# One ring of three accumulator banks in place of two and one, renewed planner durations and a new search, in a three-part attention and mixing kernel

## The chip, the cores and the metric

The kernel runs on one core of a Trainium2 chip. Its engines are TensorE (PE in the profile; PEld is its weight load), VectorE (DVE), ScalarE (ACT), GpSimd (POOL) and SyncE (SP), which issues nearly all DMAs. The metric is the device time of one execution, in microseconds, as the median of repeated runs.

## What is computed

Four batches of 448 tokens pass through causal attention with 12 heads of width 64, then a token mixer and a channel mixer, then a gated channel mix. Cut to what matters, the reference is:

```python
scores = q @ k.T / sqrt(64);  scores[mask] = -1e9          # per head, 448 x 448
attn = exp(scores - max);  attn /= sum + 1e-9
x = concat_heads(attn @ v)                                  # 4 x 448 x 768
u = x + (relu(x.T @ w_tok1) @ w_tok2).T                     # token mixing
x = u + relu(u @ w_ch1) @ w_ch2                             # channel mixing
xk, xr = lerp(x, x_prev, mu_k), lerp(x, x_prev, mu_r)
out = sigmoid(xr @ w_r) * (relu(xk @ w_k)**2 @ w_v)
```

The weights arrive in 64-bit floats. The kernel splits each into a high and a low 32-bit part and forms most products from three matmuls.

## The kernel before

**Stages.** Phase 0 does attention, token mixing and, as filler, a part of the channel mixer; it ends at about 368 us. Phase 1 does the rest of the channel mixer and the gated mix. Heads go in 24 pairs of two. For a pair, TensorE transposes q and k (tile `pt`, line 866), makes the scores (`ps`, line 891 for batch 0, line 900 with three matmuls for the others), and DVE adds the mask and finds the row maximum (line 912), ACT takes the exponential (928), DVE the reciprocal of the sum (942), DVE or POOL multiply by it (`norm`, line 946). TensorE then transposes the normalized block in five groups of four (`et_tr`, tile `pe`, line 969), ACT or DVE copies each group to SBUF (`et_copy`, recorded at line 240), TensorE forms the value product (`pv`, 985), ACT or DVE copies it to `xT`, TensorE turns it back (`pn`, 1003), and ACT and DVE split it into `xh`. After each third pair the token mixer runs: `k1` (tile `ph`), `k2` (tile `pu`) and a DVE sum into `xT` (line 1139). `early_ch1` forms the first half of the channel mixer's hidden rows (tile `pd`) for batches 0 to 2 while later pairs run; `pd` needs a whole batch's token mixing, so there is none before about 88 us.

**PSUM.** Phase 0 splits the eight banks into `ps_m` (two banks in a ring for `pt`, `pv`, `pn`, `ph`, `pu`), `ps_t` (one bank, for `pe` alone), `ps_s` (four, scores) and `ps_d` (one, `pd`). A tile that takes a bank of a ring waits until the last reader of the tile that had it before is done.

**The order.** Every step is a planner's entry: a due time, an engine (some may go to either of two), a duration, what it reads and writes, and the rings it takes from. `walk` plays all engines forward and lets each engine take, of what can start now, the entry with the lowest rank. `LAT` is the delay until a result can be used by another engine. `schedule` first shifts some ranks by pseudo-random amounts, one set per number in the list `NUDGES`, for phase 0 only. The resulting order on each engine is written into the program, and the chip's engines then run it strictly in that order, each waiting on semaphores. So the durations and the list change only which instruction stands where, and on which of two engines.

Of the kernel before, what the change touches and what calls it, by code (L numbers as in the profile page):

```python
# [10 lines left out]
F32 = mybir.dt.float32  # L11
# [4 lines left out]
PSUM = bass.MemoryType.PSUM  # L16
# [4 lines left out]
def kernel(  # L21
# [68 lines left out]


    PE, ACT, DVE, POOL, SP, NONE = "PE", "ACT", "DVE", "POOL", "SP", "-"
    LAT = {PE: 0.24, ACT: 0.2, DVE: 0.16, POOL: 0.12, SP: 2.8, NONE: 0.0}
    MODE, STICK, WAIT = 0.1, 1.5, 0.08
    DMA_RATE = 270e3

# [19 lines left out]
    def walk(mine, rank):  # L116

        for x in mine:
            x.left, x.next, x.pre = 0, [], []
        for x in mine:  # L120
            for k in x.r:
                for y in makers[k]:
                    if y.phase == x.phase:
                        x.left += 1
                        y.next.append(x)
                    else:
                        x.pre.append((None, 0.0, done_at[id(y)]))
        avail = {e: [x for x in mine if e in x.alt and not x.left] for e in free}
        out = []

        def start_of(x, eng):
            s = free[eng]
            for e, here, end in x.pre:
                s = max(s, here if e == eng != SP else end)
            if eng == PE and x.mode != state["mode"]:
                s += MODE
            more = {}
            for k in x.u:
                if k in taken:
                    continue  # L140
                pool = k[0]
                order = freed.setdefault(pool, [])
                i = len(order) + more.get(pool, 0) - bufs[pool]
                more[pool] = more.get(pool, 0) + 1
                if i >= 0:
                    ends = [done_at.get(id(y)) for y in users[order[i]]]
                    if None in ends:
                        return None
                    s = max(s, max(ends) + 0.05)
            return s  # L150

        while len(out) < len(mine):
            best = None
            for e, xs in avail.items():
                cand = [(start_of(x, e), x) for x in xs]
                cand = [c for c in cand if c[0] is not None]
                if not cand:
                    continue
                first = max(min(c[0] for c in cand), free[e]) + WAIT
                s, x = min(  # L160
                    (c for c in cand if c[0] <= first),
                    key=lambda c: rank[id(c[1])] + (STICK if e == PE and c[1].mode != state["mode"] else 0),
                )

                if any(start_of(x, o) + c < s + x.alt[e] - 0.01 for o, c in x.alt.items() if o != e):
                    others = [c for c in cand if c[1] is not x and c[0] <= first]
                    if not others:
                        continue
                    s, x = min(
                        others,  # L170
                        key=lambda c: rank[id(c[1])] + (STICK if e == PE and c[1].mode != state["mode"] else 0),
                    )
                if best is None or s < best[0]:
                    best = (s, x, e)
            assert best is not None, "stuck"
            s, x, eng = best
            for e in x.alt:
                avail[e].remove(x)
            cost = x.alt[eng]
            for k in x.u:  # L180
                if k not in taken:
                    taken[k] = s
                    freed.setdefault(k[0], []).append(k)
            free[eng] = s + cost
            end = s + cost + LAT[eng]
            if eng == PE:
                state["mode"] = x.mode
            if eng == SP:
                free[SP] = s + 0.1
                state["dma"] = max(state["dma"], s) + cost  # L190
                end = state["dma"] + LAT[SP]
            done_at[id(x)] = end
            out.append((s, x, eng))
            for y in x.next:
                y.left -= 1
                y.pre.append((eng, s + cost, end))
                if not y.left:
                    for e in y.alt:
                        avail[e].append(y)
        return out  # L200

    NUDGES = tuple(4000000 + n for n in (
# [9 lines left out]
    ))  # L214

    def noise(seed, i):
# [5 lines left out]
    def nudge(rank, mine, seed):  # L222
        share = (0.005, 0.02, 0.1)[int(3 * noise(seed, 1))]
        width = (3.0, 8.0, 20.0)[int(3 * noise(seed, 2))]
        for i, x in enumerate(mine):
            if noise(seed, 2 * i + 3) < share:
                rank[id(x)] += width * (2 * noise(seed, 2 * i + 4) - 1)

    def schedule(phase):
# [19 lines left out]
    def split64(t, key, use, dest, src, pp, n, blocks=False, lead=0):  # L249
# [52 lines left out]
        u = [("raw", k), ("tmp", k)]  # L302
        op(t - lead, SP, dma(pp * n * 8), load, w=[("raw", k)], u=u[:1])
        op(t, ACT, 0.04 + 0.43 * g, magnitude, r=[("raw", k)], w=[("mag", k)], u=u)
        slow = 0.3 if state["phase"] == 0 else 0.0
        op(t, DVE, 0.1 + (0.66 + slow) * g, shift, r=[("mag", k)], w=[("bit", k)], u=u[1:])
        op(t, DVE, 0.1 + (1.0 + slow) * g, assemble, r=[("bit", k)], w=[("asm", k)], u=u)
        op(t, ACT, 0.04 + 0.38 * g, high, r=[("asm", k)], w=[key + ("hi",)], u=u[1:] + use)
# [484 lines left out]
    with ExitStack() as c0:  # L793
# [5 lines left out]
        sp = c0.enter_context(tc.tile_pool(name="sp", bufs=4))  # L799
        ep = c0.enter_context(tc.tile_pool(name="ep", bufs=4))  # L800
        etp = c0.enter_context(tc.tile_pool(name="etp", bufs=2))
        ps_m = c0.enter_context(tc.tile_pool(name="ps_m", bufs=2, space=PSUM))
        ps_t = c0.enter_context(tc.tile_pool(name="ps_t", bufs=1, space=PSUM))
        ps_s = c0.enter_context(tc.tile_pool(name="ps_s", bufs=4, space=PSUM))
        ps_d = c0.enter_context(tc.tile_pool(name="ps_d", bufs=1, space=PSUM))
        ud = c0.enter_context(tc.tile_pool(name="ud", bufs=1))
        bufs.update({
            "kn": 2, "qn": 2, "vn": 3, "k": 2, "q": 2, "ms": 4, "e": 4, "et": 2, "xT": 6, "xh": 1,
            "h1": 1, "m": 2, "t": 1, "s": 2, "d": 1, "ue": KD, "h": 2, "st": 4,
        })  # L810

        mask = tw.tile([CP, S], F32, name="mask")
# [27 lines left out]
        def pair(g):  # L840
# [121 lines left out]
            def et_tr(i):  # L962
                if "et" not in T:
                    T["et"] = etp.tile([CP, len(groups) * S], F32, tag="et", name="et")
                pe = T["pe", i] = ps_t.tile([128, 512], F32, tag="t", name="pe")
                for j, kc in groups[i]:
                    o = place[j, kc] - S * i
                    for c in range(kc, NCH):
# [53 lines left out]
            for i, nm in enumerate("kq"):  # L1022
                t = s0 + 0.6 * i
                pt = ("m", nm, g)
                op(t, PE, 0.4, turn, nm, r=[(nm + "n", g)], w=[("pt", nm, g)], u=[(nm + "n", g), pt, (nm, g)])
                op(t - EV, ACT, 0.43, turned_hi, nm, r=[("pt", nm, g)], w=[(nm + "hi", g)], u=[pt, (nm, g)])
                if whole:
                    continue
                op(t - EV, DVE, 0.55, turned_lo, nm, r=[(nm + "hi", g)], w=[(nm + "lo", g)], u=[pt, (nm, g)])
            both = [(nm + x, g) for nm in "kq" for x in (("hi",) if whole else ("hi", "lo"))]  # L1030
            for i, cs in enumerate(units):
                t = s0 + 2.5 + (0, 2.2, 4.6)[i]
                su = ("s", i, g)
                op(
                    t, PE, (0.6, 0.74, 0.32)[i] * (4 / 3 if whole else 1), score, i, r=both, w=[("sc", i, g)],
                    u=[("k", g), ("q", g), su], mode="R",
                )
                for c in cs:
# [9 lines left out]
                            w=[("ex", j, c, g)], u=[ms, ("e", j, g), ("st", g)],  # L1048
                        )
            op(  # L1050
                s0 + 9, DVE, 0.33, recip, r=[("ex", j, c, g) for j in range(2) for c in range(NCH)],
                w=[("rc", g)], u=[("st", g)],
            )
            for j in range(2):
                for i, c in enumerate((3, 0, 1, 2)):
                    op(
                        s0 + 9.1 + 2 * j + 0.1 * i, POOL, (0.43, 0.53, 0.6, 0.7)[c], norm, j, c,
                        r=[("rc", g)], w=[("no", j, c, g)], u=[("e", j, g), ("st", g)],
                        alt={DVE: (0.16, 0.24, 0.32, 0.4)[c]},
                    )  # L1060
            for i in range(5):
                t = s0 + 11 + i
                need = [("no", j, c, g) for j, kc in groups[i] for c in range(kc, NCH)]
                op(
                    t, PE, 0.4, et_tr, i, r=need, w=[("tr", i, g)],
                    u=[("t", i, g), ("et", g)] + [("e", j, g) for j in {j for j, _ in groups[i]}],
                )
                op(
                    t - EV, ACT, 0.43, et_copy, i, r=[("tr", i, g)], w=[("et", i, g)], u=[("t", i, g), ("et", g)],
                    alt={DVE: 0.55},  # L1070
                )
            op(
# [231 lines left out]
```

## Time and profile before

| | |
|---|---|
| Median of 3 runs | 957.39 us (956.06 to 958.03) |
| Profiled execution, its own time | 957.5 us |
| Its span, first to last instruction | 955.7 us |
| TensorE busy over the span | 931.7 us (97%) |
| DVE, ACT, POOL busy | 582.7, 449.3, 67.2 us |

The profiled execution lies within the runs shown. Between its span and its own time there are 1.8 us that no instruction fills.

### The profile page before, as it was taken

Reading aid. Unit: us, or ns where it says so; the run is one execution under the profiler, and the core shown is the slowest. Engines: PE = TensorE matmul, PEld = TensorE weight load, DVE = VectorE, ACT = ScalarE, POOL = GpSimd, SP = SyncE. Lnnn points to the kernel's source line nnn. Section 1 sums busy time; section 2 is a strip of 40 time slices with the busy share of each in tenths; the row PEclk is TensorE's granted clock in tenths of the full one; section 3 lists DMA queues with packets and bytes.
Section 4 is the critical chain, followed back from the end, with each engine's and each line's share of the span. In section 5 each row is a group of like instructions: output and inputs, shape, how many; then the busy total and the mean of one; then the engine's idle time right before and its main releaser. Section 6 shows DMA issues by size and latency. Waiting matters only on the chain.

```text
span 955.7 us, 15553 instructions
## 1 busy us (share of the span) xinstructions
PE 931.7 (97%) x5496; PEld 832.2 (87%) x5496; DVE 582.7 (61%) x1450; ACT 449.3 (47%) x1082; POOL 67.2 (7%) x150
## 2 busy tenths in 40 slices
PE   6899999999999999999999999999999999999998
PEld 3566788878887888999999999999999999999998
DVE  5899998984677436997962118979745424231221
ACT  6988868774668443453430104556654313020210
POOL 1231112200111000000000000000000000000000
PEclk9999999999999999999999999999999999999999
DMA  9545565563442212566692445977741404102031
GB/s 183 132 114 140 156 172 156 168 186 103 117 124 93 81 58 98 149 185 228 204 337 102 138 151 174 308 242 240 220 141 33 150 25 154 49 19 89 28 94 50
DMA packets 149806, 133.55 MB, mean 140 GB/s; under 512 B 89888, under 2 KB 136480, under 8 KB 149728
## 3 DMA queue, kind: packets, MB, share of 16 engines
q1 hardware_dynamic: 148800, 132.33, 45.8%
q8 instruction: 43, 0.70, 0.3%
q10 hardware_dynamic: 928, 0.23, 0.1%
q14 instruction: 35, 0.29, 0.1%
HBM read 95.82 MB, written 33.03 MB: 135 GB/s over the span
## 4 chain that ended last, share of the span: by engine, by line
PE 91%; DVE 4%; ACT 3%; DMA 1%; issue 1%; SPq 0%; POOL 0%; DVEq 0%; ACTq 0%; POOLq 0%
PE pr L349 7%; PE pr L351 7%; PE pr L350 7%; PE acc L350 6%; PE acc L351 6%; PE acc L349 6%; PE pe L969 4%; PE ph L350 4%; PE ph L349 4%; PE ph L351 4%; PE pk L349 4%; PE pk L350 4%; PE pk L351 4%; PE pv L985 4%; PE ps L900 3%; PE pd L349 3%
## 5 line engine op out<-in xcount | busy, mean ns | idle before, releaser
L928 ACT ACTIVATE e<-ms,nm 112x448 f32<-112x448 f32 (+3 forms) x192 | 100.3, 526 | 13.6 <-DVE nm L912 11.6
L350 PE MATMUL acc<-a,w 128*128 128x448 f32 x288 | 105.2, 365 | 0.0
L349 PE MATMUL acc<-a,w 128*128 128x448 f32 x288 | 105.2, 365 | 0.0
L351 PE MATMUL acc<-a,w 128*128 128x448 f32 x288 | 105.2, 365 | 0.0
L912 DVE CUSTOM_DVE_ANT_0 ms<-ps,mask 112x448 f32<-112x448 f32 (+3 forms) x192 | 77.8, 442 | 6.9 <-PE ps L900 4.0
L969 PE MATMUL pe<-ident,e 112*112 112x112 f32 x480 | 69.8, 267 | 9.3 <-ACT et L240 5.2
L969 PEld LDWEIGHTS pe<-ident,e 112*112 112x112 f32 x480 | 51.2, 135 | 27.6 <-ACT et L240 6.3
L240 ACT COPY et<-pe 112x448 f32<-112x448 f32 x106 | 56.4, 532 | 37.1 <-PE pe L969 36.7
L294 ACT CAST w<-tmp 128x384 fp32r<-128x384 f32 (+2 forms) x100 | 50.1, 502 | 47.5 <-DVE tmp L289 46.8
L349 PE MATMUL pr<-w,a 128*128 128x384 f32 x216 | 72.2, 334 | 0.0
L350 PE MATMUL pr<-w,a 128*128 128x384 f32 x216 | 72.2, 334 | 0.0
L351 PE MATMUL pr<-w,a 128*128 128x384 f32 x216 | 72.2, 334 | 0.0
L534 ACT ACTIVATE a<-pk 128x448 f32<-128x448 f32 x32 | 17.5, 546 | 116.0 <-PE pk L351 116.0
L268 ACT ACTIVATE tmp<-raw 128x384 f32<-128x384 f32 (+2 forms) x100 | 54.2, 544 | 36.5 <-DVE w L298 24.5
L350 PE MATMUL pk<-a,w 128*128 128x448 f32 x192 | 70.7, 368 | 0.0
L351 PE MATMUL pk<-a,w 128*128 128x448 f32 x192 | 70.7, 368 | 0.0
L349 PE MATMUL pk<-a,w 128*128 128x448 f32 x192 | 70.6, 368 | 0.0
L572 DVE TENSOR_TENSOR r<-pr,r 128x384 f32<-128x384 f32 x28 | 15.6, 558 | 76.3 <-PE pr L351 76.2
L946 POOL TENSOR_SCALAR e<-e,rc 112x112 f32<-112x112 f32 (+3 forms) x78 | 46.7, 613 | 217.2 <-DVE rc L942 145.7
L349 PE MATMUL pd<-a,w 128*128 128x448 f32 x144 | 59.3, 412 | 0.2
L349 PE MATMUL pr<-w,kk 128*128 128x384 f32 x176 | 58.8, 334 | 0.0
L351 PE MATMUL pr<-w,kk 128*128 128x384 f32 x176 | 58.8, 334 | 0.0
(109 smaller groups left out, 2204.0 us busy)
## 6 DMA issues: line engine op xcount, KB each, us to landing
raw<-in_moe_w_ch_dram SPq DMA_DIRECT2D x48, 384.0 KB, 3.3
h_d<-he SPq DMA_DIRECT2D x24, 448.0 KB, 2.9
a<-h_d SPq DMA_DIRECT2D x24, 448.0 KB, 5.0
y<-y_d SPq DMA_DIRECT2D x48, 224.0 KB, 4.4
a<-u_d SPq DMA_DIRECT2D x36, 224.0 KB, 3.7
raw<-in_moe_w_k_dram SPq DMA_DIRECT2D x16, 384.0 KB, 4.1
raw<-in_moe_w_v_dram SPq DMA_DIRECT2D x16, 384.0 KB, 5.0
vn<-in_v_dram SPq DMA_DIRECT2D x48, 112.0 KB, 2.7
```

The lines of the kernel that those rows point to most:

```text
L240: nc.scalar.copy(o, i) if by == ACT else nc.vector.tensor_copy(o, i)
L268: nc.scalar.activation(box["tmp"], box["raw"][:, :, 1].bitcast(F32), AF.Abs, scale=65536.0)
L294: nc.scalar.copy(dest()[0], box["tmp"])
L349: nc.tensor.matmul(o, lh, rh, start=start and i == 0, stop=False)
L350: nc.tensor.matmul(o, lh, rl, start=False, stop=False)
L351: nc.tensor.matmul(o, ll, rh, start=False, stop=stop and i == n - 1)
L900: nc.tensor.matmul(T["s", j, c], T["q"][r, x, qc], T["k"][r, y, :n], start=i == 0, stop=i == 2,)
L912: nc.vector.tensor_tensor_reduce(out=ms[:, :n], in0=T["s", j, c], in1=mask[:, S - n:], scale=-0.125, scalar=BIG, op0=ALU.add, op1=ALU.min, ...
L928: nc.scalar.activation(T["e", j][:, eoff[c]:eoff[c + 1]], T["ms", j, c][:, :n], AF.Exp, bias=T["nm"][:, j, c:c + 1], scale=-1.0, accum_out ...
L946: (nc.gpsimd if by == POOL else nc.vector).tensor_scalar(out=ec, in0=ec, scalar1=T["rc"][:, j, c:c + 1], scalar2=1.0, op0=ALU.mult, op1=AL ...
L969: nc.tensor.transpose(pe[:CP, o + (c - kc) * CP:o + (c - kc + 1) * CP], T["e", j][:, eoff[c] + kc * CP:eoff[c] + (kc + 1) * CP], ident[:CP ...
L985: nc.tensor.matmul(T["pv"][64 * j:64 * j + 64, kc * CP:S], T["vn"][:, kc, j, :], T["et"][:, o:o + S - kc * CP], start=kc == 0, stop=kc == 2,)
```

## The change

The ring of two and the single bank become one ring of three: `et_tr` now takes its tile from `ps_m`, in turn with `pt`, `pv`, `pn`, `ph` and `pu`. Durations in the planner are renewed: each DMA now occupies SP's issue for 0.5 us (1.0 us for the loads of q, k, v and u) instead of 0.1, the first pair's transposes and scores are taken as slower, the split of a weight in phase 0 as faster on DVE, and `norm` on DVE as slower by 0.07 to 0.15. The list of rank shifts is another one (76 numbers in place of 118), and steps due before -10 (the first loads) are no longer shifted.

```diff
-    LAT = {PE: 0.24, ACT: 0.2, DVE: 0.16, POOL: 0.12, SP: 2.8, NONE: 0.0}
+    LAT = {PE: 0.24, ACT: 0.2, DVE: 0.16, POOL: 0.12, SP: 2.6, NONE: 0.0}
...
-                free[SP] = s + 0.1
+                free[SP] = s + (1.0 if x.f[0].__name__ == "load" and x.u[0][0] != "raw" else 0.5)
...
-    NUDGES = tuple(4000000 + n for n in (
+    NUDGES = tuple(1000000 + n for n in (
...
-            if noise(seed, 2 * i + 3) < share:
+            if x.t > -10 and noise(seed, 2 * i + 3) < share:
...
-        slow = 0.3 if state["phase"] == 0 else 0.0
+        slow = 0.12 if state["phase"] == 0 else 0.0
...
-        ps_m = c0.enter_context(tc.tile_pool(name="ps_m", bufs=2, space=PSUM))
-        ps_t = c0.enter_context(tc.tile_pool(name="ps_t", bufs=1, space=PSUM))
+        ps_m = c0.enter_context(tc.tile_pool(name="ps_m", bufs=3, space=PSUM))
...
-            "h1": 1, "m": 2, "t": 1, "s": 2, "d": 1, "ue": KD, "h": 2, "st": 4,
+            "h1": 1, "m": 3, "s": 2, "d": 1, "ue": KD, "h": 2, "st": 4,
...
-                pe = T["pe", i] = ps_t.tile([128, 512], F32, tag="t", name="pe")
+                pe = T["pe", i] = ps_m.tile([128, 512], F32, tag="m", name="pe")
...
-                op(t, PE, 0.4, turn, nm, r=[(nm + "n", g)], w=[("pt", nm, g)], u=[(nm + "n", g), pt, (nm, g)])
+                op(t, PE, 0.9 if g == 0 else 0.4, turn, nm, r=[(nm + "n", g)], w=[("pt", nm, g)], u=[(nm + "n", g), pt, (nm, g)])
...
-                    t, PE, (0.6, 0.74, 0.32)[i] * (4 / 3 if whole else 1), score, i, r=both, w=[("sc", i, g)],
+                    t, PE, (0.6, 0.74, 0.32)[i] * (1.8 if g == 0 else 4 / 3 if whole else 1), score, i, r=both, w=[("sc", i, g)],
...
-                s0 + 9, DVE, 0.33, recip, r=[("ex", j, c, g) for j in range(2) for c in range(NCH)],
+                s0 + 9, DVE, 0.45, recip, r=[("ex", j, c, g) for j in range(2) for c in range(NCH)],
...
-                        alt={DVE: (0.16, 0.24, 0.32, 0.4)[c]},
+                        alt={DVE: (0.24, 0.31, 0.42, 0.55)[c]},
...
-                    u=[("t", i, g), ("et", g)] + [("e", j, g) for j in {j for j, _ in groups[i]}],
+                    u=[("m", "t", i, g), ("et", g)] + [("e", j, g) for j in {j for j, _ in groups[i]}],
```

On TensorE's queue in the first pairs, before, a group of `pe` (four transposes) mostly stands alone between other work; `ps` are scores, `pt` the transposes of q and k, `pv` the value product, `pn` the turn back:

```order
L985 MATMUL pv<-et,vn 64x224 x2
L969 MATMUL pe<-ident,e 112x112 x4
L891 MATMUL ps<-kt,qt 112x224 x2
L1003 MATMUL pn<-ident,xT 112x128 x4
L969 MATMUL pe<-ident,e 112x112 x4
L866 MATMUL pt<-ident,kn 128x112 x4
L969 MATMUL pe<-ident,e 112x112 x4
L866 MATMUL pt<-ident,qn 128x112 x4
L969 MATMUL pe<-ident,e 112x112 x4
L891 MATMUL ps<-kt,qt 112x448 x2
L969 MATMUL pe<-ident,e 112x112 x4
```

At the same place of the changed kernel (lines stand 5 lower) all five groups of the second pair follow each other:

```order
L980 MATMUL pv<-et,vn 64x224 x2
L886 MATMUL ps<-kt,qt 112x448 x2
L886 MATMUL ps<-kt,qt 112x336 x2
L886 MATMUL ps<-kt,qt 112x112 x2
L998 MATMUL pn<-ident,xT 112x128 x4
L964 MATMUL pe<-ident,e 112x112 x20
L886 MATMUL ps<-kt,qt 112x224 x2
L861 MATMUL pt<-ident,kn 128x112 x4
L861 MATMUL pt<-ident,qn 128x112 x4
L980 MATMUL pv<-et,vn 64x448 x2
```

So runs of transposes are longer. Counted over phase 0, TensorE's queue goes 120 times into or out of a run of scores or of value products before, and 108 times in the changed kernel; between transposes and the wide matmuls (`ph`, `pu`, `pd`) it goes 162 times before and 135 times after. The count of matmuls is the same, 5256.

At TensorE's border between the phases, before, nine matmuls of the channel mixer (`ph` from line 349 to 351, first three blocks of u) stand ahead of the last token-mixing product `pu`:

```order
L351 MATMUL pu<-w_129,h_4787 128x448
L349 MATMUL ph<-a,w 128x448
L350 MATMUL ph<-a,w 128x448
L351 MATMUL ph<-a,w 128x448
L349 MATMUL ph<-a,w 128x448
L350 MATMUL ph<-a,w 128x448
L351 MATMUL ph<-a,w 128x448
L349 MATMUL ph<-a,w 128x448
L350 MATMUL ph<-a,w 128x448
L351 MATMUL ph<-a,w 128x448
L349 MATMUL pu<-w_129,h_4787 128x448
```

In the changed kernel all 18 of the last `pu` come first and the channel mixer follows without a break:

```order
L345 MATMUL pu<-w_126,h_4788 128x448
L346 MATMUL pu<-w_126,h_4788 128x448
L347 MATMUL pu<-w_126,h_4788 128x448
L345 MATMUL ph<-a,w 128x448
L346 MATMUL ph<-a,w 128x448
L347 MATMUL ph<-a,w 128x448
```

So the last product whose sum the channel mixer waits for stands nine matmuls earlier against it.

On SP's queue at the start, before, a weight load is issued ahead of the first q:

```order
L261 DMA raw<-in_moe_w_tok_dram 112x512
L855 DMA qn<-in_q_dram 112x4x64
L855 DMA kn<-in_k_dram 112x4x64
L855 DMA vn<-in_v_dram 112x4x64 x2
L261 DMA raw<-in_moe_w_tok_dram 112x512
```

In the changed kernel k and q come first, and TensorE's first transposes are those of k:

```order
L850 DMA kn<-in_k_dram 112x4x64
L850 DMA qn<-in_q_dram 112x4x64
L257 DMA raw<-in_moe_w_tok_dram 112x512
L850 DMA vn<-in_v_dram 112x4x64 x2
L257 DMA raw<-in_moe_w_tok_dram 112x512
```

So the loads that the first transposes wait for stand one place earlier. Of the steps that may go to either of two engines, POOL has 94 `norm` and 18 weight subtractions in place of 78 and 15, DVE 98 `norm` in place of 114, 6 copies to `xT` in place of 1, and 11 of `et` in place of 14. In phase 1 the last 2599 matmuls stand in the same order in both.

## Rows read from the trace of the kernel before

**Rows 1.** The page: engines' busy time, and the group that copies `pe`.
```profile
PE 931.7 (97%) x5496; PEld 832.2 (87%) x5496; DVE 582.7 (61%) x1450; ACT 449.3 (47%) x1082; POOL 67.2 (7%) x150
...
L240 ACT COPY et<-pe 112x448 f32<-112x448 f32 x106 | 56.4, 532 | 37.1 <-PE pe L969 36.7
```

**Rows 2.** Stretches: length, busy us of PE, PEld, DVE, ACT, POOL; clock, DMA.
```profile
0.00:25.00 25.00, 15.80 (x76) 10.28 (x76) 14.46 (x55) 15.50 (x44) 3.78 (x13) 0.89 0.88 175
25.00:50.00 25.00, 20.73 (x147) 12.28 (x145) 20.98 (x77) 22.68 (x71) 6.66 (x10) 0.97 0.54 139
...
75.00:100.00 25.00, 22.73 (x186) 17.56 (x184) 24.16 (x75) 19.73 (x57) 5.04 (x8) 1.00 0.45 110
100.00:350.00 250.00, 248.08 (x1793) 205.90 (x1791) 183.70 (x547) 170.65 (x468) 38.27 (x60) 1.00 0.45 133
...
370.00:950.00 580.00, 580.00 (x3022) 550.15 (x3021) 306.79 (x613) 193.49 (x375) 4.51 (x44) 1.00 0.46 146
950.00:956.00 6.00, 1.35 (x8) 1.03 (x6) 0.56 (x1) 0.00 (x0) 0.00 (x0) 0.90 0.16 37
```

**Rows 3.** Waits of TensorE: us in total, times, longest.
```profile
PE pe L969 <- ACT et L240: 5.2, 9, 1.1
PE pt L866 <- DMA qn<-in_q_dram: 5.1, 1, 5.1
PE pe L969 <- DVE e L946: 3.4, 5, 1.2
...
PE pe L969 <- POOL e L946: 0.3, 1, 0.3
```

**Rows 4.** Timeline, the start: SP's first issues and TensorE's first transposes.
```profile
0.73 0.41 SPq L261 DMA_DIRECT2D raw<-in_moe_w_tok_dram  x1
1.21 0.41 SPq L855 DMA_DIRECT2D qn<-in_q_dram  x1
...
5.07 0.98 PE L866 MATMUL pt<-ident,qn 112*128 112x112 f32 x4 [5.07 <-DMA qn<-in_q_dram]
```

**Rows 5.** Timeline, three rows of TensorE and ACT at 84 us.
```profile
84.23 0.60 PE L969 MATMUL pe<-ident,e 112*112 112x112 f32 x4 [0.24 <-ACT et L240]
84.86 0.53 ACT L240 COPY et<-pe 112x448 f32<-112x448 f32 x1 [0.25 <-PE pe L969]
85.45 0.59 PE L969 MATMUL pe<-ident,e 112*112 112x112 f32 x4 [0.62 <-ACT et L240]
```

**Rows 6.** Timeline of TensorE at 251 and 255 us, starts of runs.
```profile
251.01 0.55 PE L866 MATMUL pt<-ident,kn 112*128 112x112 f32 x4
251.39 0.55 PE L866 MATMUL pt<-ident,qn 112*128 112x112 f32 x4
251.87 1.59 PE L900 MATMUL ps<-kt,qt 64*112 64x448 f32 x18
...
255.36 0.55 PE L969 MATMUL pe<-ident,e 112*112 112x112 f32 x4
...
255.97 0.36 PE L350 MATMUL pd<-a,w 128*128 128x448 f32 x1
256.16 0.36 PE L351 MATMUL pd<-a,w 128*128 128x448 f32 x1
```

**Rows 7.** Timeline of TensorE at the border of the phases.
```profile
367.49 0.47 PE L349 MATMUL ph<-a,w 128*128 128x448 f32 x1 [0.70 <-ACT a L1192]
368.15 0.47 PE L350 MATMUL ph<-a,w 128*128 128x448 f32 x1 [0.19 <-DVE a L1199]
```

**Rows 8.** Timeline, `norm` on DVE and POOL together at 171, and at 251 us.
```profile
170.79 3.33 DVE L946 TENSOR_SCALAR e<-e,rc 112x336 f32<-112x336 f32 x5
170.95 1.45 POOL L946 TENSOR_SCALAR e<-e,rc 112x112 f32<-112x112 f32 x3 [4.26 <-DVE rc L942]
...
173.66 0.57 PE L969 MATMUL pe<-ident,e 112*112 112x112 f32 x4 [0.78 <-DVE e L946]
...
251.37 2.08 DVE L946 TENSOR_SCALAR e<-e,rc 112x224 f32<-112x224 f32 x6 [0.46 <-DVE rc L942]
```

More of the change, by code (lines that the diff above doesn't have):

```diff
@@ L1065, in pair @@
                     t, PE, 0.4, et_tr, i, r=need, w=[("tr", i, g)],
-                    u=[("t", i, g), ("et", g)] + [("e", j, g) for j in {j for j, _ in groups[i]}],
+                    u=[("m", "t", i, g), ("et", g)] + [("e", j, g) for j in {j for j, _ in groups[i]}],
                 )
                 op(
-                    t - EV, ACT, 0.43, et_copy, i, r=[("tr", i, g)], w=[("et", i, g)], u=[("t", i, g), ("et", g)],
+                    t - EV, ACT, 0.43, et_copy, i, r=[("tr", i, g)], w=[("et", i, g)], u=[("m", "t", i, g), ("et", g)],
                     alt={DVE: 0.55},
```

14 rows, old and new, of the table NUDGES are left out of this document.

## The prediction, on record before the result

> **What bounds the kernel now.** I read the page's busy times first, then the stretches, then TensorE's waits, and last the timeline at the places where those waits lie. TensorE is busy for 931.7 of 955.7 us [rows 1], so all the idle time there is to win is 24.0 us. The stretches show where it lies [rows 2]. From 370 to 950 us TensorE is busy without a gap, 580.0 of 580 us; its last 2599 matmuls keep their order, so this part can only be shifted. After its last matmul at 951.35 us (1.35 us of the last stretch are busy) 4.35 us of output remain, which nothing in the change touches. Before the first matmul lie 5.07 us [rows 4]. That leaves 24.0 - 4.35 - 5.07 = 14.6 us of gaps, nearly all before 100 us: 25 - 15.80 - 5.07 = 4.1 us in the first stretch, 4.3 in the second, 2.3 from 75 to 100; the 250 us after that hold only 1.9 [rows 2], since there the matmuls `pd` fill what attention leaves free.
>
> The waits say what ended the gaps [rows 3]: nine waits of the transposes `pe` for an ACT copy, 5.2 us together, and five for `norm` on DVE, 3.4 us. The first kind is seen at 84 us [rows 5]: a group of `pe` starts at 84.23, its copy runs on ACT from 84.86 for 0.53 us, and only then, at 85.45, after 0.62 us of idling, the next group can write into the single bank. One group is thus possible each 1.22 us, where its transposes alone would need 0.38 (four at the rate of 251.01 to 251.39 [rows 6]).
>
> **The change part by part.** All terms are differences to the profiled execution's own 957.5 us, which stands 0.1 us above the median of 957.39; the 1.8 us around its span are taken as fixed.
>
> The start. SP issues a weight load at 0.73 us and the first q half at 1.21; TensorE waits for q until 5.07 [rows 4]. In the changed order the two halves that SP loads stand first and the weight third, so the load that ends this wait goes out 0.48 us earlier. The weight is late by about two issues, but its split on DVE runs while TensorE makes the first scores. If the landing were set by ACT's queue, nothing would come of it. I take -0.5 (bounds 0 and -0.5).
>
> The runs on TensorE. Four transposes and the entry into scores take 251.87 - 251.39 = 0.48 us, where four transposes in a row take 0.38 [rows 6]: an edge costs 0.10. I take the same for leaving, and for value products. Edges go from 120 to 108: 12 x 0.10 = -1.2. Between transposes and wide matmuls, a run of four and the first `pd` take 255.97 - 255.36 = 0.61 us; without edges it were 0.38 + 0.19 (the next `pd`, 255.97 to 256.16) = 0.57. So a run costs 0.04, and 162 - 135 = 27 edges fewer are 13.5 runs: -0.5. Together -1.7. Where an edge lies in a gap it saves nothing, so the bounds are -0.9 and -1.7; I take -1.6, since most of them stand after 100 us, where there are almost no gaps.
>
> The single bank. The 5.2 us for ACT's copies can go: with three banks, three groups may run one behind the other (0.38 us each) while the copies follow at 0.53 us each. But a run of twenty transposes outruns ACT: the fourth group must wait for the first copy, and ACT's queue holds exponentials ahead of it. ACT is busy for 22.68 of 25 us in the second stretch [rows 2]. Bounds 0 and -5.2; I take half, -2.6.
>
> The border of the phases. The channel mixer waited 0.70 + 0.19 us for the high and low part of the last sum [rows 7], because nine of its matmuls stood ahead of the last `pu`. In the changed order all `pu` precede them; these nine and six more matmuls of earlier blocks, 15 x 0.20 = 3.0 us, now cover the sum, the high part and the low part (three steps over one tile; ACT copies one in 0.53 us [rows 5], so about 1.6 us and the handovers). Bounds 0 and -0.9; I take -0.9.
>
> `norm` on POOL. Sixteen of them, and three weight subtractions, go from DVE to POOL. DVE was busy 24.16 of 25 us from 75 to 100 [rows 2], so it gains room, but POOL is slower. The waits of `pe` for `norm` were 3.4 + 0.3 us [rows 3] with 78 on POOL; in proportion to 94 they become 3.7 x 94 / 78 = 4.5: +0.8. Bounds: -1.9 (half of them go, because DVE has room) and +3.7 (they double).
>
> A view of this cost is the place at 171 us [rows 8]: while POOL does three `norm` in 1.45 us, DVE needs 3.33 us for five, and TensorE then waits 0.78 us; at 251 us DVE does six in 2.08, 0.35 each. The five would have taken 1.75, so 1.6 us were lost, about as long as POOL was at work. [...]
>
> The shared ring. What `pe` leaves on its own bank it now takes from the others: a late reader of any `pt`, `pv` or `pn` holds up all. No row of before shows such a wait. Nearest are the nine on the single bank; bounds 0 and +5.2. With 9 fillings for a pair, most held for a transpose run and one 0.53 us copy, three banks are well short of full where a pair takes some 15 us (24 pairs in 368 us). I take 0. The remaining renewed durations only choose the order already counted.
>
> Sum: -0.5 - 1.6 - 2.6 - 0.9 + 0.8 = -4.8; 957.5 - 4.8 = **952.7 us**.
>
> **The rivals.** [...] With the waits for `norm` doubled (+3.7 in place of +0.8) the time is 952.7 + 2.9 = 955.6, no measurable change; this has 0.10.
>
> Second, the change does little: the copies were late because ACT was full, so 5.2 us stay, and only the start, the runs and the border come: 957.5 - 0.5 - 1.6 - 0.9 + 0.8 = 955.3, or 956.2 if the border also stays. For it speaks ACT's 91% in the second stretch, against it the 0.25 us for which ACT itself idled before the copy at 84.86 [rows 5]. 0.11.
>
> Third, on the other side: the shared ring stalls TensorE in each pair. Place: a transpose run whose bank is still held by a `pt` or `pn` that needs both ACT and DVE, with ACT in the midst of exponentials. A price of 0.4 us for each of 24 pairs is +9.6: 962.3. It decides from 6.7 us on (4.8 eaten up and 1.9 more), 0.28 us for each pair. Against it: after 100 us neither ACT nor DVE is full, 170.65 and 183.70 of 250 us [rows 2]. 0.14.
>
> Fourth, more comes than I count: all of the 5.2 goes and `norm` brings none: 957.5 - 0.5 - 1.6 - 5.2 - 0.9 = 949.3. That wants ACT and DVE both ahead of TensorE in the first 100 us. 0.13.
>
> **How the numbers follow.** The forecast has 0.52, its own range is 950.5 to 955.4: single bank from -1 to -4, `norm` from -0.5 to +1.5. About 0.2%, 1.9 us, is what a measurement of this kernel can tell from no change, so faster means below 955.5. Faster: 0.52 + 0.13 = 0.65; same: 0.10 + 0.11 = 0.21; slower: 0.14. The range of 949.5 to 957.6 leaves out the third rival and about half of the fourth, 0.20 together.
>
> **What would show it.** In the changed profile: first transposes at about 4.6 us; TensorE's waits of `pe` for ACT's copies at 2 to 3 us in place of 5.2; no wait at the border; waits for `norm` near 4.5 us; TensorE's gaps between first and last matmul near 11.5 us in place of 14.6; the dense part of 580 us unchanged. I am wrong if `pt`, `pv` or `pn` wait for ACT or DVE by more than some 3 us in all, if `norm` on POOL ends most waits, or if the dense part shows gaps, since DVE's and ACT's order there moves too.

## The result, and the profile after

The changed kernel takes 946.25 us (946.15 to 946.51, four runs), the kernel before 957.57 in the same series: a ratio of 0.989 with a 95% interval of 0.9875 to 0.9905. Forecast were 952.7 us and a range of 949.5 to 957.6. The direction was right, the gain of 11.3 us more than twice the 4.8 forecast, and it lies outside the range. The profiled execution takes 946.25 us, its span is 944.5.

The page of the changed kernel has this line of busy time, as [rows 1]:

```profile
PE 928.7 (98%) x5496; PEld 832.4 (88%) x5496; DVE 581.1 (62%) x1433; ACT 445.4 (47%) x1080; POOL 75.9 (8%) x169
```

Its stretches, with the columns of [rows 2]:

```profile
0.00:25.00 25.00, 18.73 (x114) 11.42 (x115) 15.65 (x59) 18.16 (x55) 7.62 (x18) 1.00 1.03 199
25.00:50.00 25.00, 21.09 (x146) 14.20 (x145) 23.17 (x75) 21.88 (x67) 9.68 (x17) 0.93 0.54 141
50.00:75.00 25.00, 23.80 (x170) 18.07 (x170) 23.54 (x69) 20.78 (x59) 7.56 (x12) 1.00 0.56 150
75.00:100.00 25.00, 25.00 (x201) 20.46 (x200) 22.69 (x75) 18.34 (x56) 5.23 (x8) 1.00 0.39 106
100.00:350.00 250.00, 249.94 (x1806) 208.90 (x1801) 183.83 (x537) 169.00 (x468) 41.23 (x70) 1.00 0.46 130
350.00:370.00 20.00, 20.00 (x101) 18.55 (x100) 14.59 (x31) 8.46 (x17) 0.00 (x0) 1.00 0.31 101
370.00:940.00 570.00, 570.00 (x2972) 540.82 (x2970) 297.12 (x592) 188.77 (x364) 4.53 (x44) 1.00 0.46 147
```

The span is 11.2 us shorter. 1.0 of it is the earlier first matmul (4.03 in place of 5.07 us, below). TensorE's busy time falls by 931.7 - 928.7 = 3.0. The rest, 7.2, are gaps between its first and last matmul: 944.5 - 928.7 = 15.8 us idle, less 4.03 at the start and the same 4.35 at the end, leave 7.4 us, where before there were 14.6. After 75 us TensorE now hardly stops: 25.00 of 25 and 249.94 of 250 us, against 22.73 and 248.08 in [rows 2]. The dense part is as it was.

TensorE's waits, as [rows 3], all that the view lists:

```profile
PE pt L861 <- DMA kn<-in_k_dram: 4.0, 1, 4.0
PE pe L964 <- POOL e L941: 2.5, 4, 1.7
PE ps L886 <- ACT qt L865: 1.3, 2, 0.7
PE pe L964 <- DVE e L941: 1.1, 1, 1.1
PE pv L980 <- ACT et L236: 0.8, 1, 0.8
PE pe L964 <- DVE xh L1007: 0.6, 1, 0.6
PE pe L964 <- DVE et L236: 0.3, 1, 0.3
PE ph L345 <- ACT et L236: 0.2, 1, 0.2
PE pt L861 <- DMA qn<-in_q_dram: 0.2, 1, 0.2
```

No transposes `pe` wait for ACT's copies any more; of the 5.2 us in [rows 3], 1.0 comes back as `pv` and `ph` waiting for a copy, and 0.3 as `pe` waiting for a copy on DVE. The 0.6 us that `pe` waits for `xh` are a wait for a bank of the ring, since `pe` does not read `xh`. Waits for `norm` are 3.6 us in place of 3.7, but now 2.5 of them are for POOL. The waits at the border [rows 7] are gone.

The largest gap left is seen on TensorE's timeline at 25 to 32 us:

```profile
24.81 0.65 PE L998 MATMUL pn<-ident,xT 128*112 128x128 f32 x4
27.18 0.31 PE L964 MATMUL pe<-ident,e 112*112 112x112 f32 x1 [1.72 <-POOL e L941]
28.54 3.66 PE L964 MATMUL pe<-ident,e 112*112 112x112 f32 x19 [1.05 <-DVE e L941]
```

One transpose stands between two waits for `norm`, and after them the run of 19 takes 3.66 us, 0.19 each, twice the 0.095 of [rows 6]: the granted clock was 0.50 from 29 to 32 us and 1.00 from 33 us on, which is the 0.93 of the second stretch.

### The profile page after: what moved, and what is told of

It is laid out like the page before. It is cut to its first block, busy times and chain, and to the rows that moved or that the text cites. A ratio compares the mean times of both kernels' runs of the same rounds, so it can differ in the third digit from the quotient of the medians.

```text
span 944.5 us, 15602 instructions
## 1 busy us (share of the span) xinstructions
PE 928.7 (98%) x5496; PEld 832.4 (88%) x5496; DVE 581.1 (62%) x1433; ACT 445.4 (47%) x1080; POOL 75.9 (8%) x169
## 4 chain that ended last, share of the span: by engine, by line
PE 95%; ACT 2%; DVE 2%; POOL 1%; issue 0%; DMA 0%; SPq 0%; POOLq 0%; ACTq 0%
PE pr L347 7%; PE pr L345 7%; PE pr L346 7%; PE acc L346 6%; PE acc L347 6%; PE acc L345 6%; PE pe L964 5%; PE ph L345 4%; PE ph L346 4%; PE ph L347 4%; PE pv L980 4%; PE pk L346 4%; PE pk L345 4%; PE pk L347 4%; PE ps L895 4%; PE pd L345 3%
## 5 line engine op out<-in xcount | busy, mean ns | idle before, releaser
L530 ACT ACTIVATE a<-pk 128x448 f32<-128x448 f32 x32 | 17.5, 546 | 120.7 <-PE pk L347 120.6
L236 ACT COPY et<-pe 112x448 f32<-112x448 f32 x109 | 53.6, 541 | 35.1 <-PE pe L964 34.9
L941 POOL TENSOR_SCALAR e<-e,rc 112x224 f32<-112x224 f32 (+3 forms) x94 | 53.0, 580 | 211.0 <-DVE rc L937 132.9
L964 PE MATMUL pe<-ident,e 112*112 112x112 f32 x480 | 62.0, 267 | 4.9 <-POOL e L941 2.5
L426 ACT ACTIVATE a<-ph 128x448 fp32r<-128x448 f32 x24 | 13.1, 546 | 98.4 <-PE ph L347 92.9
```

Source lines behind the costliest of these rows:

```text
L236: nc.scalar.copy(o, i) if by == ACT else nc.vector.tensor_copy(o, i)
L941: (nc.gpsimd if by == POOL else nc.vector).tensor_scalar(out=ec, in0=ec, scalar1=T["rc"][:, j, c:c + 1], scalar2=1.0, op0=ALU.mult, op1=AL ...
L964: nc.tensor.transpose(pe[:CP, o + (c - kc) * CP:o + (c - kc + 1) * CP], T["e", j][:, eoff[c] + kc * CP:eoff[c] + (kc + 1) * CP], ident[:CP ...
```

## The experiments

Ratios are to the kernel before, run on the same chip in turn, with their 95% intervals. First the parts of the change one by one.

**The ring alone, at the old order.** Every engine keeps its order; only the banks are one ring, and the planner does not know it.

```diff
-        ps_m = c0.enter_context(tc.tile_pool(name="ps_m", bufs=2, space=PSUM))
-        ps_t = c0.enter_context(tc.tile_pool(name="ps_t", bufs=1, space=PSUM))
+        ps_m = c0.enter_context(tc.tile_pool(name="ps_m", bufs=3, space=PSUM))
...
-                pe = T["pe", i] = ps_t.tile([128, 512], F32, tag="t", name="pe")
+                pe = T["pe", i] = ps_m.tile([128, 512], F32, tag="m", name="pe")
```

> The kernel before with its own order on every engine, only the banks are one ring of three. If the freedom of the banks itself is the gain, the 5.2 us of waits for ACT's copies go and the time is 952.5 or less. If the gain needs another order, so that transposes stand where the new banks let them run, the time stays within 1.5 us of before, 956 to 959. If the shared ring harms by itself, it is over 960.

Measured: 956.24 us, ratio 0.9993 (0.9972 to 1.0014): no change, as the second of the three cases expected. Its longest waits of TensorE:

```profile
PE pt L865 <- DMA qn<-in_q_dram: 5.2, 1, 5.2
PE pe L968 <- ACT et L240: 1.6, 3, 0.6
PE pe L968 <- DVE e L945: 1.5, 4, 0.7
PE pt L865 <- DMA kn<-in_k_dram: 1.1, 1, 1.1
```

The waits for copies do fall, from 5.2 to 1.6, and those for `norm` on DVE from 3.4 to 1.5. But the time does not follow: another wait appears at the start, for the load of k (1.1 us), and TensorE's clock is low for longer. Its stretch from 30 to 42 us, and the same of the kernel before:

```profile
30.00:42.00 12.00, 10.40 (x52) 5.76 (x54) 10.67 (x37) 9.71 (x28) 4.95 (x8) 0.72 0.54 151
```

```profile
30.00:42.00 12.00, 9.48 (x72) 5.63 (x68) 11.08 (x40) 11.23 (x36) 4.84 (x7) 1.00 0.63 177
```

With a granted clock of 0.72 it is busy longer than before (10.40 against 9.48 us) and does fewer matmuls (52 against 72).

**The ring with a new plan, the old list of shifts.** The planner knows the ring; durations and list are those of before. Beside the banks as above:

```diff
...
-            "h1": 1, "m": 2, "t": 1, "s": 2, "d": 1, "ue": KD, "h": 2, "st": 4,
+            "h1": 1, "m": 3, "s": 2, "d": 1, "ue": KD, "h": 2, "st": 4,
...
```

> The ring known to the planner, old durations and the old list of shifts, which was chosen for the other rings. Ring theory: 949 to 953. Search theory (the list is worth most, and only for the plan it was chosen for): 956 to 962.

983.26 us, 1.0265 (1.0223 to 1.0307): far slower, beyond both expectations. The same plan without any list takes 966.4 us (below), so a list chosen for one plan costs some 17 us on another. Here the ring does stall TensorE. `pe` reads neither `kt` nor `xh`, but it waits until DVE has read them out of `pt` and `pn`, which hold the ring's banks:

```profile
PE pe L968 <- DVE kt L873: 2.8, 2, 2.4
...
PE pe L968 <- DVE xh L1011: 1.6, 1, 1.6
```

**No shifts at all**, for the four combinations of ring and durations. The edit in each is this, on the kernel before or after, or with one of the two parts put back:

```diff
-    NUDGES = tuple(4000000 + n for n in (
...
+    NUDGES = ()
```

Nothing of the change:

> The kernel before without any shifts of ranks. Search theory: the list is worth 5 to 10 us, 962 to 968. Ring theory: the list is worth little, 957 to 960.

Ring and renewed durations:

> The changed kernel without any shifts: ring and durations alone. Ring theory: 946 to 951, most of the 11 us stays. Search theory: 955 to 962, most of it is gone.

The ring alone, known to the planner:

> The kernel before with the ring known to the planner and no shifts. Against the kernel before without shifts this is the ring's own worth with a free order. Ring theory: 4 to 8 us faster than that kernel. If durations matter more, 0 to 2 us.

Renewed durations alone:

> The changed kernel without shifts and with banks two and one: renewed durations alone. Ring theory: within 2 us of the kernel before without shifts. If the durations are what helps, 4 to 8 us faster than that kernel.

| without shifts | two and one bank | ring of three |
|---|---|---|
| old durations | 962.3, 1.0055 (1.0030 to 1.0079) | 966.4, 1.0104 (1.0077 to 1.0131) |
| renewed durations | 961.8, 1.0055 (1.0025 to 1.0084) | 965.0, 1.0088 (1.0053 to 1.0124) |

Without a list neither part helps, and the ring comes out 3 to 4 us slower, with intervals that touch or overlap. So the theory that the ring or the durations by themselves carry the gain fell here: the changed kernel without its list is slower than the kernel before, and than either expectation for it. Its list is worth 965.03 - 946.25 = 18.8 us, that of before 962.33 - 957.39 = 4.9. Stretches of the changed kernel without its list:

```profile
75.00:100.00 25.00, 24.24 (x190) 20.29 (x187) 24.21 (x75) 16.05 (x50) 5.20 (x8) 1.00 0.33 83
100.00:350.00 250.00, 244.60 (x1756) 202.19 (x1754) 179.98 (x528) 168.55 (x466) 38.39 (x59) 1.00 0.45 133
```

From 100 to 350 us it has 5.4 us of gaps, where the changed kernel has 0.06.

**The new list on two and one bank**, planned again:

```diff
-        ps_m = c0.enter_context(tc.tile_pool(name="ps_m", bufs=3, space=PSUM))
+        ps_m = c0.enter_context(tc.tile_pool(name="ps_m", bufs=2, space=PSUM))
+        ps_t = c0.enter_context(tc.tile_pool(name="ps_t", bufs=1, space=PSUM))
...
```

> The changed kernel with banks two and one, planned again with its durations and its list. Ring theory: 952 to 958, the waits for copies come back, about 5 us. If durations and list carry the gain whatever the banks, 946 to 949.

965.96 us, 1.0099 (1.0071 to 1.0127), above both expectations. The same plan without a list takes 961.8, so here too the list does not fit the plan. This run and the ring with the old list cannot say what the ring is worth.

**The first loads**, by the rule that steps due before -10 keep their ranks, on the kernel before:

```diff
-            if noise(seed, 2 * i + 3) < share:
+            if x.t > -10 and noise(seed, 2 * i + 3) < share:
```

> The kernel before, and only the first loads (due before -10) keep their ranks, so that k and q go out before the weight. If the start is a term of its own, the first transposes start near 4.1 us in place of 5.1 and the time falls by 0.5 to 1.0, to 956.6 to 957.0. If work on DVE and ACT sets the first stretch, the start moves and the time does not, 957.5.

956.84 us, 1.0003 (0.9989 to 1.0018), and the edit did not do what it was meant to: the weight, due at -9, is still shifted and still goes first, and only k and q change places. The first issues and the first transposes:

```profile
0.73 0.40 SPq L261 DMA_DIRECT2D raw<-in_moe_w_tok_dram  x1
...
4.99 0.98 PE L866 MATMUL pt<-ident,kn 112*128 112x112 f32 x4 [4.99 <-DMA kn<-in_k_dram]
```

In the changed kernel, with the weight third:

```profile
0.73 0.40 SPq L850 DMA_DIRECT2D kn<-in_k_dram  x1
...
4.03 0.98 PE L861 MATMUL pt<-ident,kn 112*128 112x112 f32 x4 [4.03 <-DMA kn<-in_k_dram]
```

So with the weight ahead the first landing is 1.0 us later, twice the 0.48 us of its issue. What that is worth by itself was not measured.

**One search for all four.** What a search makes of ring and durations can only be compared if it is the same search. For each combination 40,000 numbers were tried in turn, each kept where the planner's own end of phase 0 fell; steps due before -10 keep their ranks in all four. The edit is the list again:

```diff
+    NUDGES = tuple(7000000 + n for n in (
...
```

> Ring of three, renewed durations, and a list found anew by one and the same search for four kernels (40,000 numbers tried in turn from another start, each kept where the planner's own end of phase 0 falls). If the changed kernel's time is what such a search gives with this ring and these durations, 944 to 949. If its list was a lucky one, 950 or more.

> The same search for renewed durations with banks two and one. If the ring is needed, because a search can only use banks that are there: 951 to 957, with some 5 us of waits for ACT's copies. If better durations are what makes a search worth more on the chip: 945 to 950.

> The same search for the ring with the old durations. If the ring is what counts: 946 to 951. If durations are what counts: 954 to 960, about as before, the waits being others than the planner reckoned with.

> The same search for the kernel before: banks two and one, old durations. If the old list was no worse than another: 954 to 961. If the gain is only a longer or luckier search: 946 to 951.

| after one search | two and one bank | ring of three |
|---|---|---|
| old durations | 955.2, 0.9982 (0.9967 to 0.9998) | 956.4, 0.9989 (0.9966 to 1.0012) |
| renewed durations | 954.1, 0.9971 (0.9954 to 0.9987) | 946.9, 0.9900 (0.9875 to 0.9924) |

Either part alone brings next to nothing; the 1.1 us of the renewed durations with two and one bank are about what its first transposes start earlier (4.1 in place of 5.1 us). Both together bring 8.3 us against the kernel with neither (955.2 - 946.9), and about as much as the changed kernel, whose list is therefore no lucky one. So the gain comes from ring and renewed durations together, by way of the order that a search makes of them. Each cell rests on one list. Two lists for one planner differ by 3.4 us further down, so the 8.3 stand clear of that, and differences of 1 us between cells do not. The difference is not one of the clock alone either: at a mean granted clock of 0.995 the kernel with both took 947.70 us, the other three from 953.13 to 955.41.

With two and one bank the wait for ACT's copies stays whatever the durations; with the old ones it is 3.9 us, with renewed ones

```profile
PE pe L964 <- ACT et L235: 6.6, 12, 1.3
```

That wait is not the whole difference. From this kernel (span 952.4 us, TensorE busy 932.0) to the one with ring and renewed durations (945.7, busy 927.6) TensorE's idle time falls by 2.3 us and its busy time by 4.4.

With the ring but old durations, the copies are hardly waited for (0.3 us), yet the kernel is 9.5 us slower than with renewed ones. Little of that is idle time: spans of 955.4 and 945.7 us less busy times of 935.3 and 927.6 leave 20.1 and 18.1 us idle, 2.0 of 9.7. The other 7.7 are busy time, and most of it lies where the clock is low. Its stretches:

```profile
0.00:25.00 25.00, 18.39 (x96) 11.92 (x96) 15.57 (x58) 16.13 (x47) 3.48 (x12) 0.93 0.90 185
25.00:50.00 25.00, 19.97 (x118) 13.98 (x120) 20.55 (x75) 21.17 (x64) 6.55 (x9) 0.78 0.41 105
50.00:75.00 25.00, 23.23 (x154) 16.94 (x150) 21.17 (x65) 18.00 (x55) 6.47 (x9) 0.94 0.53 145
```

Counted as time at granted clocks of 1.00 and 0.50, the two seen in the changed kernel at 25 to 36 us, these are by estimate 3.5 + 11.0 + 3.0 = 17.5 us at half speed. With renewed durations the same stretches have 0.93, 1.00 and 1.00, or 3.5 us. The 14 us more are worth up to 7.0 us, if TensorE had work in all of them. From 42 to 54 us of the kernel with old durations (stretch), and rows of its timeline there:

```profile
42.00:54.00 12.00, 11.30 (x53) 7.25 (x55) 7.50 (x25) 7.50 (x23) 1.89 (x4) 0.57 0.59 139
```

```profile
41.29 0.31 PE L962 MATMUL pe<-ident,e 112*112 112x112 f32 x1 [1.01 <-ACT kt L863]
42.27 0.31 PE L962 MATMUL pe<-ident,e 112*112 112x112 f32 x1 [0.67 <-POOL e L939]
43.01 3.65 PE L962 MATMUL pe<-ident,e 112*112 112x112 f32 x18 [0.43 <-POOL e L939]
...
49.30 3.87 PE L978 MATMUL pv<-et,vn 112*64 112x448 f32 x16
```

The same with renewed durations:

```profile
42.00:54.00 12.00, 12.00 (x90) 9.15 (x89) 11.22 (x39) 11.78 (x40) 4.33 (x6) 1.00 0.49 125
```

```profile
43.54 2.11 PE L980 MATMUL pv<-et,vn 112*64 112x448 f32 x16
```

One value product takes 3.87 us in place of 2.11. ACT, busy for 7.5 of 12 us, waits 4.5 us for TensorE, and DVE 1.6 for ACT. Where this low clock begins, TensorE does only two single transposes between waits of 1.01, 0.67 and 0.43 us, the first for a bank of the ring out of which ACT still copied `kt`, the others for `norm` on POOL. The split of 2.0 and 7.7 says where the time lies in these two executions, not what the kernel would take at full clock: at 0.995 and 0.996 the kernel with old durations took 955.25 and 953.11 us, still over 5 us more than the one with renewed durations at 0.995.

**Which durations.** Under the ring, one group was put back at a time, with the same search each.

```diff
-                free[SP] = s + (1.0 if x.f[0].__name__ == "load" and x.u[0][0] != "raw" else 0.5)
+                free[SP] = s + 0.1
```

> Ring and renewed durations, but SP's issue and landing delay as before, and the same search. If loads that come too late are what spoils the ring under the old durations: 952 to 957, with waits for q, k, v or u. If not: 946 to 949.

942.84 us, 0.9857 (0.9830 to 0.9885).

```diff
-                        alt={DVE: (0.24, 0.31, 0.42, 0.55)[c]},
+                        alt={DVE: (0.16, 0.24, 0.32, 0.4)[c]},
```

> Ring and renewed durations, but norm on DVE and the reciprocal as short as before, and the same search. If the planner's too fast norm spoils the ring (DVE gets too many, transposes wait for them, and TensorE's clock falls in these gaps): 951 to 957, with more than 4 us of waits for norm on DVE. If not: 946 to 949.

947.27 us, 0.9907 (0.9879 to 0.9935).

```diff
-                op(t, PE, 0.9 if g == 0 else 0.4, turn, nm, r=[(nm + "n", g)], w=[("pt", nm, g)], u=[(nm + "n", g), pt, (nm, g)])
+                op(t, PE, 0.4, turn, nm, r=[(nm + "n", g)], w=[("pt", nm, g)], u=[(nm + "n", g), pt, (nm, g)])
...
-        slow = 0.12 if state["phase"] == 0 else 0.0
+        slow = 0.3 if state["phase"] == 0 else 0.0
```

> Ring and renewed durations, but the first pair's transposes and scores and the weight split as before, and the same search. If the start, planned too early or too late, spoils the ring: 950 to 955, and gaps before 50 us. If not: 946 to 949.

950.74 us, 0.9943 (0.9921 to 0.9965). And with the last group alone renewed:

> Ring, and of the renewed durations only the first pair's transposes and scores and the weight split; SP and norm as before; the same search. If these durations are what makes the ring usable: 943 to 949. If each of the three groups is needed or helps in part: 950 to 956.

950.02 us, 0.9921 (0.9887 to 0.9954). So SP's issue and `norm` can each stay old without loss. In both cases the first expectation fell: neither spoils the ring, and with SP's old durations the time lies even below the second. The first pair's durations and the weight split alone bring part. What it costs when they stay old is open. The 950.74 us are the median of ten runs, five at 946.9 to 949.3 and five at 952.2 to 954.4, and the profiled one (952.23) lost time where the change does nothing. From 460 to 600 us, with the same matmuls in the same order, it did 679 of them, the changed kernel 692 (stretch of each):

```profile
460.00:600.00 140.00, 140.00 (x679) 127.17 (x678) 63.21 (x131) 34.09 (x66) 0.40 (x4) 1.00 0.55 184
460.00:600.00 140.00, 140.00 (x692) 129.78 (x691) 65.72 (x137) 36.00 (x70) 0.50 (x5) 1.00 0.57 189
```

How the gain divides among the groups stays open too, because one list differs from another, as the next two show.

**Other lists.** A search three times as long for the changed kernel, and another list for the kernel with SP's old durations:

> The changed kernel with a list from a search three times as long (120,000 numbers). The planner's end of phase 0 falls by some 4 us more than for the changed kernel. If the planner's gain is the chip's: 942 to 944. If what is left are waits that the planner does not see, no faster than the changed kernel: 946 to 949.

945.47 us, 0.9889 (0.9858 to 0.9920), between the two ranges. The ratio is that of the changed kernel (0.9890): what the planner gained further did not arrive.

> As p1 (SP's old issue durations), with a list from another start of the search, whose planned end is 1.9 us later. If the old SP durations are better for the chip: 942 to 945. If one list differs from another by this much: 946 to 949.

946.21 us, 0.9889 (0.9852 to 0.9927). With another list it was 942.84; both have the same planner, and their intervals overlap. Of all versions the one at 942.84 is fastest, 1.4% below the kernel before, and in its profiled execution TensorE's granted clock is 1.00 in every stretch up to 350 us (the first two):

```profile
0.00:25.00 25.00, 18.10 (x98) 10.62 (x100) 16.56 (x62) 17.97 (x53) 6.13 (x16) 1.00 1.02 203
25.00:50.00 25.00, 22.04 (x169) 14.10 (x166) 22.80 (x80) 24.02 (x74) 9.31 (x16) 1.00 0.54 140
```

## Why the prediction was wrong, point by point

**The start** was forecast at -0.5 and measured -1.0. Moving the weight behind k and q gave more than the 0.48 us of its issue; that its transfer stood in their way was not shown. A size.

**The runs on TensorE**: -1.6 forecast, -3.0 of busy time measured. The sum left out the clock, though [rows 2] showed it. Before, it was 0.50 from 20 to 25 us and 1.00 from 30 to 50 us. A mean of 0.89 and 0.97 over two stretches of 25 us is then 5.5 + 1.5 = 7.0 us at half speed, 0.93 in the changed kernel 3.5 us; 3.5 us less at half speed are, by estimate, up to 1.75 us. The ring at the old order gives a check on this price: it has the same instructions in the same order, two stretches of 25 us at 0.86 and 0.93 and so 10.5 us at half speed, and TensorE is busy for 933.4 us, 1.7 more than before. By this estimate some 1.7 of the 3.0 are the clock and 1.3 the edges, of which no run measured the price alone. Not all of the clock's part need come from the change: the kernel before, profiled at a mean clock of 0.996, reached 0.998 in other runs and then mostly took 954.3 to 956.3 us, against 946.2 for the changed kernel at 0.998.

**The single bank** was the step that failed. I took half of its 5.2 us, with ACT's load as the reason that copies would be late again. In the changed kernel TensorE's waits for copies went from 5.2 to 1.0 on ACT (`pv` and `ph`) and 0.3 on DVE, 3.9 less where I had 2.6. ACT was no obstacle. But neither is it true that the ring gives these microseconds: at the old order it brought no measurable change, although the waits fell to 1.6.

**The step behind it that failed** reads "The remaining renewed durations only choose the order already counted". That order was counted by adding up its visible places, each wait of before lowered or kept. The gaps between first and last matmul fell by 7.2 us, where the terms for copies, border and `norm` made 2.7. Besides the copies, waits that I had carried over unchanged also went:

```profile
PE ps L891 <- ACT e L928: 1.3, 1, 1.3
PE pt L866 <- DVE xh L1012: 1.0, 1, 1.0
PE pn L1003 <- ACT xT L240: 0.8, 1, 0.8
```

The changed kernel waits nowhere for `ps` banks held by an exponential, nor for `xT` ahead of `pn`, and 0.6 us for `xh`. The table after one search shows that neither ring nor durations bring this, only a search with both; by which places in the order it does so stays open. The fourth rival's 949.3, the lowest time I named, took gaps of two kinds away; in truth several kinds fell together, and the time at half clock with them.

**The border** was right: -0.9, no wait left there.

**`norm` on POOL** was forecast at +0.8 and came out at -0.1 (3.6 against 3.7 us). The doubled waits behind the 955.6 did not come, though after the first load `norm` is now the largest kind left. That POOL's three `norm` cost DVE the 1.6 us at 171 us was not tested by a run, and my reading of [rows 8] was incomplete. Nearly all of the 1.6 us lies in one `norm` on DVE, which ended at 173.51 us, 0.14 us after POOL's weight subtraction, an instruction of 1.00 us behind the three `norm`:

```profile
171.58 1.93 DVE L946 TENSOR_SCALAR e<-e,rc 112x224 f32<-112x224 f32 x1
...
172.37 1.00 POOL L298 TENSOR_TENSOR w<-tmp,w 128x384 fp32r<-128x384 f32 x1
```

And the six at 251 us are no measure of DVE beside an idle POOL, since POOL did two `norm` there too, in 1.06 us.

**The rivals.** The first two (955.6 and 955.3), at which the time would stand still, needed waits that did not come. The third, stalls of the shared ring, hardly came in the changed kernel (0.6 us of `pe` for `xh`, at most 1.0 us of `pv` and `ph` for copies). It is not fiction, though: with the old list `pe` waited 4.4 us for `kt` and `xh`. That no row of before shows such a wait was misread: the 1.0 us of `pt` for `xh` above is one, on the ring of two. The fourth was nearest, and too timid. The forecast's own range is mis-added as well: its bounds for the single bank and `norm` give 950.0 to 955.0, not 950.5 to 955.4.

## What to carry to other kernels

Where a planner sets the order, a change of its resources, its durations and its search must be judged together: here each of the first two alone was worth about nothing after the same search, and both 8.3 us. An old list of shifts says nothing of a new resource. And a forecast that adds up the waits of the old order holds for that order; with a new search its lower end should lie well below that, towards the sum of all gaps, plus what the clock gives back.

## What the runs showed of the hardware

Fewer waits for copies came together with a lower granted clock of TensorE in two kernels with the ring. At the old order these waits fell from 5.2 to 1.6 us, and from 30 to 42 us the clock was 0.72 in place of 1.00. With the old durations after one search they were 0.3 us; a value product took 3.87 us where the clock from 42 to 54 us was 0.57, and 2.11 us with renewed durations, where it was 1.00. Of the 9.7 us between the profiled spans of these last two kernels, 7.7 were busy time, by estimate up to 7.0 of it by the low clock, and only 2.0 idle. At that fall of the clock TensorE idled for 1.01, 0.67 and 0.43 us, and only the first wait was for a bank. What makes the clock fall was not shown: the kernel before idled 0.62 us for its single bank at 84 us, and from 75 to 950 us the mean clock of its stretches is 1.00 [rows 2, 5].

A `norm` of 224 columns on DVE took 1.93 us beside work on POOL. In the same kernel the six during which POOL was idle took 0.32 to 0.33 us, and the 23 others beside POOL 0.32 to 0.72 us.

The same matmuls in the same order at a granted clock of 1.00 took 2% longer in one execution than in another (679 against 692 in 140 us). Its cause stays open.
